# Plain attention steps that divide after the value products, with sums made by products with a block of ones, and a new table of order

## The chip, the cores and the metric

One core of a Trainium2 chip runs the program. The metric is the device time of one execution, in microseconds. Five engines work side by side, each on its own queue and in the order of that queue: PE (TensorE: matrix products; its weight loads are shown as PEld), DVE (VectorE), ACT (ScalarE), POOL (GpSimd) and SP (SyncE, which only issues transfers). They wait for each other by semaphores.

## The reference, cut to what matters

Causal attention with a bias from a running sum, and behind it a feed-forward layer whose hidden value is the largest of three products. B = 8 batches, H = 8 heads, S = 576 positions, D = 64; the feed-forward part has 4608 tokens, width 512 and 768 hidden values.

```python
scores = scale * np.matmul(q, k.transpose(0, 1, 3, 2))
s_pos = np.maximum(s, 0.0)
cum = np.cumsum(s_pos, axis=-1)
bias = -(cum[:, :, :, None] - cum[:, :, None, :])
scores = np.where(causal, -1000000000.0, scores + np.minimum(bias, 0.0))
scores = scores - np.max(scores, axis=-1, keepdims=True)
attn = np.exp(scores)
attn = attn / (np.sum(attn, axis=-1, keepdims=True) + 1e-09)
out = np.matmul(attn, v)
...
h = np.maximum(np.maximum(x @ w1, x @ w2), x @ w3)
return (h @ w_out).astype(np.float32)
```

## The kernel before

Heads go in pairs, one head on each half of the 128 partitions. A visit is one pair with some of its query blocks of 128 rows, and a step is one query block of one visit: 160 steps. The first four visits (v = 0 to 3, steps 0 to 7, query blocks 0 and 1 of batch 0) are the plain steps: they work in 32-bit floats throughout, with one product where all later steps split every number into two 16-bit halves and make three. The change touches the plain steps alone, besides the order.

One turn of the main loop, step t, puts on the queues: what is left of the probabilities of step t (`plain_probs`); the row maxima of step t+1 (`highest`, DVE, L771); the products of the feed-forward layer that are due; the scores of step t+2 (PE, L686 to L697); the exponentials of step t+1 (`expo`, ACT, L797, tiles e); and a list of other work for this step. In the plain steps these are, in the old code: the sums of the exponentials, which ACT collects beside L797 and rounds off at L803 (tile se); their reciprocal on DVE (L877, tile ri); two diagonal matrices with it (L880, ACT, tiles dg); products of the exponentials with them, which transpose and divide at once (L886, PE, tiles pp); a copy out of PSUM (L892, ACT, tiles p); the value products (L901, PE, into the accumulator av); and after each second step a copy of the result (L919, ACT) into x, the input of the feed-forward layer. L919 and its like are put off by a list, `pending`, that the next turn empties.

Beside the plain steps the weights of the feed-forward layer arrive (24 tiles of 512 KB, tiles r) and are unpacked from 64-bit floats by four operations: L1043 on ACT (tiles t), and L1047, L1051 and L1057 on DVE. `column_sums` then makes sums of them on PE (L1069), also into av; their largest value (L1077, tile amwu, DVE) leads by way of L536 to a scale, with which L1110 (ACT) and L1115 (DVE) split the weights into halves (tiles w). As soon as x is there, the up products of the first set (L1222, PE, tiles pm, in groups of 8 products), their maxima (L1234, DVE, tiles h) and the down products (L1244, PE, tiles po) run. All later sets run as L1142, L1159 and L1184.

The order of it all is written out by hand in a table, PLAN: `moved` shifts single pieces of work by whole steps, GROUPS says how many groups of feed-forward products run in the middle and at the end of each step, `fetched` when a weight is loaded, and KEEP adds products whose result nobody uses (`keep_on`, L928: weights identb, into av) at given steps.

Of the kernel before, what the change touches and what calls it, by code (L numbers as in the profile page):

```python
# [21 lines left out]
"moved": ({('later_keys',): 1, ('load', 10): 2, ('load', 4): -2, ('load', 5): -2, ('load', 6): -3, ('load', 7): -5, ('load_v',  # L22
19): -1, ('load_v', 20): 1, ('load_v', 24): 1, ('load_v', 29): 1, ('load_v', 32): 1, ('load_v', 34): 2, ('load_v',
37): 2, ('load_v', 5): -1, ('load_v', 7): -2, ('nat_bias', 18, 1): -1, ('nat_bias', 23, 0): -1, ('nat_bias', 30, 0):
1, ('nat_bias', 34, 0): 1, ('nat_bias', 38, 0): 2, ('nat_hi', 22, 0): -1, ('nat_hi', 25, 0): -1, ('nat_hi', 26, 1): 1,
('nat_hi', 30, 0): -1, ('nat_hi', 30, 1): 1, ('nat_hi', 34, 0): -1, ('nat_hi', 38, 0): -1, ('nat_hi', 38, 1): 1,
('nat_own', 21, 0, 0): 1, ('nat_own', 21, 0, 1): 2, ('nat_own', 21, 1, 0): 2, ('nat_own', 21, 1, 1): 2, ('nat_own',
22, 0, 0): 2, ('nat_own', 22, 0, 1): 1, ('nat_own', 25, 0, 0): 1, ('nat_own', 25, 0, 1): 1, ('nat_own', 25, 1, 0): 2,
('nat_own', 25, 1, 1): 1, ('nat_own', 26, 0, 0): 2, ('nat_own', 26, 0, 1): 1, ('nat_own', 26, 1, 0): 2, ('nat_own',
26, 1, 1): 1, ('nat_own', 29, 0, 0): 1, ('nat_own', 29, 0, 1): 1, ('nat_own', 29, 1, 0): 1, ('nat_own', 29, 1, 1): 2,  # L30
('nat_own', 30, 0, 1): 2, ('nat_own', 30, 1, 1): 2, ('nat_own', 33, 0, 0): 2, ('nat_own', 33, 0, 1): 1, ('nat_own',
33, 1, 1): 2, ('nat_own', 34, 0, 1): 2, ('nat_own', 34, 1, 0): 2, ('nat_own', 34, 1, 1): 2, ('nat_own', 37, 0, 1): 2,
('nat_own', 37, 1, 1): 2, ('nat_own', 38, 0, 0): 1, ('nat_own', 38, 0, 1): 1, ('nat_own', 38, 1, 0): 2, ('nat_own',
38, 1, 1): 1, ('pair_max', 20, 0): 1, ('pair_max', 21, 0): 2, ('pair_max', 22, 1): 1, ('pair_max', 23, 0): 2,
('pair_max', 23, 1): 1, ('pair_max', 24, 0): 1, ('pair_max', 24, 1): 1, ('pair_max', 25, 0): 1, ('pair_max', 27, 0):
1, ('pair_max', 28, 0): 1, ('pair_max', 28, 1): 1, ('pair_max', 29, 0): 2, ('pair_max', 30, 0): 3, ('pair_max', 30,
1): 3, ('pair_max', 31, 0): 1, ('pair_max', 31, 1): 1, ('pair_max', 32, 0): 1, ('pair_max', 33, 1): 1, ('pair_max',
34, 0): 2, ('pair_max', 34, 1): 3, ('pair_max', 35, 0): 2, ('pair_max', 36, 0): 1, ('pair_max', 36, 1): 1,
('pair_max', 37, 1): 1, ('pair_max', 38, 0): 2, ('pair_max', 38, 1): 2, ('pair_max', 39, 0): 2, ('pair_max', 39, 1):
1, ('pair_scale3', 3): 1, ('prep2', 10): 1, ('prep2', 9): -1, ('prep3', 5): -2, ('prep3', 7): 2, ('prep3', 8): -1,  # L40
('prep5', 11): 1, ('prep5', 15): -1, ('prep5', 17): -1, ('prep5', 18): -1, ('prep5', 4): -1, ('prep5', 7): -1,
('vmax', 20): 1, ('vmax', 21): 2, ('vmax', 22): 2, ('vmax', 24): 2, ('vmax', 25): 1, ('vmax', 26): 2, ('vmax', 30): 1,
('vmax', 32): 1, ('vmax', 33): 2, ('vmax', 34): 2, ('vmax', 36): 1, ('vmax', 37): 2, ('load_nat', 34): 1, ('decode4',
10): 1, ('prep3', 15): 1, ('nat_far', 29, 0, 1): -1, ('nat_far', 38, 0, 0): 1, ('nat_own', 24, 1, 1): 1, ('nat_bias',
37, 1): -1, ('nat_far', 23, 1, 1): -1, ('nat_own', 39, 0, 1): 1, ('nat_far', 24, 0, 1): -1, ('nat_far', 18, 1, 0): 1,
('load_nat', 31): 1, ('load_nat', 26): -2, ('nat_far', 38, 1, 0): 1, ('load_nat', 28): -2, ('nat_hi', 24, 0): 1,
('prep2', 0): -3, ('decode4', 21): 2, ('prep4', 22): -1, ('decode3', 17): -1, ('load_nat', 27): 1, ('nat_bias', 25,
1): 1, ('prep2', 11): 1, ('vmax', 39): 1, ('nat_bias', 22, 1): 2, ('load_v', 31): 1, ('load_nat', 36): -1,
('nat_bias', 35, 1): -2, ('nat_far', 35, 1, 1): 1, ('nat_bias', 38, 1): 1, ('nat_bias', 29, 1): 1, ('prep4', 24): -1,
('prep5', 14): -1, ('nat_hi', 16, 0): -1, ('prep5', 38): 1, ('nat_own', 31, 0, 1): 1, ('nat_hi', 28, 0): 1,  # L50
('nat_far', 32, 1, 0): -1, ('nat_far', 35, 0, 0): -1, ('bias4', 0): 1, ('prep4', 35): -2, ('load_w', 7): 1, ('nat_hi',
27, 0): -1, ('nat_bias', 24, 0): 2, ('prep3', 6): -1, ('prep5', 24): -1, ('load_nat', 35): -2, ('load_nat', 39): 1,
('nat_own', 35, 1, 0): 2, ('nat_hi', 33, 0): 1, ('nat_bias', 23, 1): 2, ('nat_far', 31, 1, 1): -1, ('prep4', 23): 1,
('nat_far', 29, 1, 0): -1, ('prep4', 15): -1, ('load_v', 22): -1, ('load_v', 10): 1, ('nat_far', 35, 1, 0): -2,
# [1526 lines left out]
```

## Time and profile before

| | |
|---|---|
| time before, median of 3 runs | 832.24 us (832.12 to 832.46) |
| the profiled execution: its time | 831.47 us |
| its span, first to last instruction | 829.7 us |
| PE busy | 799.0 us (96%) |
| PEld busy | 621.1 us (75%) |
| DVE busy | 634.9 us (77%) |
| ACT busy | 531.1 us (64%) |
| POOL busy | 299.2 us (36%) |
| mean granted TensorE clock | 0.991 |

An engine is busy while it works on an instruction. The shares are means over the whole span; which engine holds the others up has to be read stretch by stretch. The granted clock is the share of TensorE's full 2.4 GHz; its other level is 1.2 GHz, so that 0.66 over a stretch is a mixture of the two.

### The profile page before, as it was taken

How to read it: one execution, taken by the hardware profiler on the slowest of the kernel's cores; microseconds unless marked ns; L12 is line 12 of the kernel's file. 1: busy time of each engine (PE TensorE's matmuls, PEld its weight loads, DVE VectorE, ACT ScalarE, POOL GpSimd, SP SyncE). 2: the span in 40 equal slices, each digit the busy share in tenths (PEclk: the TensorE clock that was granted, in tenths of full speed). 3: DMA queues.
4: the chain of work that ended last, by engine and by line, in shares of the span. 5: the costliest groups of instructions: out<-in, count | busy, mean ns of one | idle time of the engine just before them, and what ended most of it. 6: DMA issues, size and time to landing. Idle time of an engine off the chain costs nothing.

```text
span 829.7 us, 20468 instructions
## 1 busy us (share of the span) xinstructions
PE 799.0 (96%) x7705; PEld 621.1 (75%) x7705; DVE 634.9 (77%) x1560; ACT 531.1 (64%) x1458; POOL 299.2 (36%) x531
## 2 busy tenths in 40 slices
...
GB/s 351 389 89 95 87 206 207 147 176 156 146 175 156 143 160 178 163 137 174 148 182 136 156 140 190 122 141 123 164 175 92 139 123 121 96 67 70 14 13 32
DMA packets 232387, 119.86 MB, mean 144 GB/s; under 512 B 204512, under 2 KB 213216, under 8 KB 232288
## 3 DMA queue, kind: packets, MB, share of 16 engines
...
q10 hardware_dynamic: 576, 1.57, 0.5%
...
## 4 chain that ended last, share of the span: by engine, by line
PE 85%; DVE 8%; ACT 3%; DMA 2%; issue 1%; DVEq 0%; ACTq 0%
PE pm L1142 47%; PE po L1184 15%; PE av L1008 8%; PE s L662 6%; DMA r<-in_w_dram 2%; PE pm L1222 2%; PE s L674 2%; DVE prl L855 1%; PE s L717 1%; DVE w L1115 1%; PE po L1244 1%; PE s L737 1%; ACT t L1043 1%; ACT prh L852 1%; DVE am L547 1%
## 5 line engine op out<-in xcount | busy, mean ns | idle before, releaser
L1142 PE MATMUL pm<-x,w 128*128 128x320 f16 (+1 forms) x3240 | 422.2, 287 | 2.4 <-ACT x L1018 0.7
L1142 PEld LDWEIGHTS <-w 128*128 128x128 f16 x3240 | 312.4, 98 | 91.9 <-issue 5.3
L1159 DVE SCALAR_TENSOR_TENSOR m<-pm,m 128x320 f32<-128x320 f32 (+1 forms) x180 | 81.7, 456 | 96.6 <-PE pm L1142 84.4
L1148 POOL CAST hh<-m 128x320 f16<-128x320 f32 (+1 forms) x90 | 46.7, 518 | 289.9 <-DVE m L1159 223.6
L852 ACT ACTIVATE prh<-e,ri 128x384 f16<-128x384 f32 (+2 forms) x192 | 91.1, 522 | 85.3 <-DVE ri L827 84.7
L1184 PE MATMUL po<-hh,w 128*128 128x320 f16 (+1 forms) x720 | 140.3, 287 | 0.0
L1184 PEld LDWEIGHTS <-w 128*128 128x128 f16 x1080 | 103.8, 98 | 29.6 <-issue 1.3
L766 DVE CUSTOM_DVE_ANT_0 s<-s,later,qf 128x128 f32<-128x128 f32 (+1 forms) x192 | 103.6, 550 | 9.5 <-PE s L662 6.8
L797 ACT ACTIVATE e<-s,nm 128x128 f32<-128x128 f32 (+4 forms) x216 | 105.4, 496 | 4.6 <-DVE nm L766 2.0
L855 DVE SCALAR_TENSOR_TENSOR prl<-e,ri,prh 128x384 f16<-128x384 f32 (+2 forms) x192 | 102.7, 575 | 3.1 <-ACT prh L852 2.2
L1184 PE MATMUL po<-hl,w 128*128 128x320 f16 (+1 forms) x360 | 103.2, 287 | 0.0
L276 POOL COPY lh<-fixed 64x576 f16<-64x576 f16 x96 | 73.6, 780 | 78.2 <-DVE fixed L251 76.2
L1156 ACT ACTIVATE m<-pm 128x320 f32<-128x320 f32 (+1 forms) x90 | 36.3, 403 | 73.7 <-PE pm L1142 71.6
L1149 POOL TENSOR_TENSOR hl<-m,hh 128x320 f16<-128x320 f32 (+1 forms) x90 | 69.6, 773 | 7.4
L662 PE MATMUL s<-lh 128*128 128x128 f16 (+3 forms) x384 | 67.1, 299 | 1.3 <-DVE prl L855 1.3
L1008 PEld LDWEIGHTS <-vh 128*64 128x64 f16 x1312 | 54.5, 111 | 11.9 <-issue 11.3
L1195 ACT ACTIVATE o<-po,os 128x320 f32<-128x320 f32 (+1 forms) x60 | 29.9, 498 | 50.1 <-PE po L1184 42.2
L797 ACT ACTIVATE s<-s,nm 128x512 f32<-128x512 f32 (+1 forms) x72 | 48.6, 674 | 0.0
L251 DVE SCALAR_TENSOR_TENSOR fixed<-fixed,qf,fixed 128x576 f16<-128x576 f32 x48 | 41.6, 902 | 6.3 <-ACT fixed L247 6.1
L662 PEld LDWEIGHTS <-lh 128*128 128x128 f16 x384 | 34.2, 98 | 15.5 <-POOL hl L1149 1.5
L797 ACT ACTIVATION_READ_ACCUMULATOR e<-s,nm 128x1 f32 x216 | 43.9, 203 | 0.0
L852 ACT ACTIVATE prh<-s,ri 128x512 f16<-128x512 f32 x48 | 30.3, 683 | 21.0 <-DVE ri L827 20.9
(196 smaller groups left out, 1184.4 us busy)
## 6 DMA issues: line engine op xcount, KB each, us to landing
...
```

Source lines behind the costliest of these rows:

```text
L276: nc.gpsimd.tensor_copy(out=R[v]["h"][own, j, x], in_=staged(v)[own, 3 - x])
L662: nc.tensor.matmul(ps[:, j, :nk], lhsT=w[:, c, qs], rhs=w[:, 1 - c, 0:nk], start=(x == "h" and not (lone and j)), stop=(x == "l"), skip_gr ...
L766: nc.vector.tensor_tensor_reduce(out=sc[:, j], in0=sc[:, j], in1=future[0][:, Q4 - nk:Q4], scale=n, scalar=3.0e38, op0=ALU.add, op1=ALU.mi ...
L797: nc.scalar.activation(out=to, in_=sc, func=AF.Exp, bias=nm[:, j:j + 1], scale=-1.0 if below(t) else 1.0, accum_out=sm[:, j:j + 1],)
L852: nc.scalar.activation(out=hi, in_=src, func=AF.Copy, scale=sc)
L855: nc.vector.scalar_tensor_tensor(out=lo, in0=src, scalar=sc, in1=hi, op0=ALU.mult, op1=ALU.subtract)
L1008: nc.tensor.matmul(o if ph else o.rearrange("p (i c) -> p i c", c=P), lhsT=lt, rhs=rt, start=(n < 2), stop=(n >= len(todo) - 2), skip_grou ...
L1142: nc.tensor.matmul(pm[:, :nq], lhsT=w[:, wt, kt, :], rhs=xt, start=(n == 0), stop=(n == 3 * NKT - 1))
L1148: nc.gpsimd.tensor_copy(out=st["hh"][:, ft, :nq], in_=m1[:, :nq])
L1149: nc.gpsimd.tensor_tensor(out=st["hl"][:, ft, :nq], in0=m1[:, :nq], in1=st["hh"][:, ft, :nq], op=ALU.subtract)
L1159: nc.vector.scalar_tensor_tensor(out=m1[:, :nq], in0=pm[:, :nq], scalar=HSC, in1=m1[:, :nq], op0=ALU.mult, op1=ALU.max)
L1184: nc.tensor.matmul(pm[:, :nq], lhsT=W[18 + ft][:, wt, dt, :], rhs=st[ht][:, ft, :nq], start=(n == 0), stop=(n == 3 * NFT - 1),)
```

## The change

In the plain steps the division moves behind the value products. ACT no longer collects sums beside the exponentials, and L803, L877 and L880 go. The products that transpose (pp) take the constant identity matrix in place of the diagonals. Behind the value products of each step, PE multiplies the same transposed probabilities by a block of ones of 64 columns (`pick`), which leaves the sums of each head in 64 rows of av, beside the values. ACT copies them, with 1e-9 added, into a tile rs (`norm`, put off as L919 was); after each second step DVE takes the reciprocal of rs over 256 columns and multiplies av by it into x (`out`), which takes the place of L919. KEEP is emptied, which takes out eight products, and some 55 entries of `moved`, GROUPS and `fetched` change by one or two steps, nearly all behind the plain steps. Line numbers behind the plain steps grow by eight.

```diff
--- before.py
+++ after.py
...
-"KEEP": ({('b', 37): 2, ('b', 70): 6}),
+"KEEP": ({}),
...
@@ -458,6 +461,10 @@
         nc.gpsimd.memset(blk[r, r], 1.0)
     one = const.tile([P, 1], BF16, name="one")
     nc.gpsimd.memset(one, 1.0)
+    pick = const.tile([P, D], F32, name="pick")
+    eps = const.tile([P, 1], F32, name="eps")
+    nc.gpsimd.memset(pick, 1.0)
+    nc.gpsimd.memset(eps, EPS)
     ones = const.tile([P, 2], F32, name="ones")
     nc.gpsimd.memset(ones, 0.0)
     sel = io.tile([HB, 1, 2, 160], F32R, tag="raw", name="sel", bufs=2)
@@ -780,8 +787,9 @@
     def expo(t):
         ps, nm, nk = U[t]
         nj = 2 if nk < S else 1
-        sm = small.tile([P, 2], F32, tag="sm", name=f"sm{t}")
         plain = steps[t][0] < NPA
+        if not plain:
+            sm = small.tile([P, 2], F32, tag="sm", name=f"sm{t}")
         away = not plain and aside(t)
         if away:
             E[t] = moe.tile([P, 2, 512], F32, tag="ex", name=f"e{t}", bufs=2)
@@ -796,11 +804,12 @@
                 to = E[t][:, j, :nk] if nj == 2 else E[t].rearrange("p j c -> p (j c)")[:, 0:S]
             nc.scalar.activation(
                 out=to, in_=sc, func=AF.Exp, bias=nm[:, j:j + 1], scale=-1.0 if below(t) else 1.0,
-                accum_out=sm[:, j:j + 1],
+                **({} if plain else dict(accum_out=sm[:, j:j + 1])),
             )
+        if plain:
+            return
         se = small.tile([P, 2], F32, tag="se", name=f"se{t}")
-        psc = 1.0 if plain else PSC
-        nc.scalar.activation(out=se[:, :nj], in_=sm[:, :nj], func=AF.Copy, scale=1.0 / psc, bias=EPS / psc)
+        nc.scalar.activation(out=se[:, :nj], in_=sm[:, :nj], func=AF.Copy, scale=1.0 / PSC, bias=EPS / PSC)
         SE[t] = (se, nj)
 
     PT = {}
@@ -871,26 +880,22 @@
     def plain_probs(t):
         v, qb = steps[t]
         U.pop(t)
-        se, _ = SE.pop(t)
         e = E.pop(t)
-        ri = small.tile([P, 2], F32, tag="ri", name=f"ri{t}")
-        nc.vector.reciprocal(out=ri, in_=se)
-        dg = att.tile([P, 2, P], F32, tag="vh", name=f"dg{t}")
-        for j in range(2):
-            nc.scalar.activation(out=dg[:, j], in_=ident, func=AF.Copy, scale=ri[:, j:j + 1])
         yield
         pm = ps_m.tile([P, 512], F32, tag="m", name=f"pp{t}")
         for kb in range(qb + 1):
             for j in range(2):
                 o = (2 * kb + j) * P
                 nc.tensor.matmul(
-                    pm[:, o:o + P], lhsT=e[:, j, kb * P:(kb + 1) * P], rhs=dg[:, j], start=True, stop=True
+                    pm[:, o:o + P], lhsT=e[:, j, kb * P:(kb + 1) * P], rhs=ident, start=True, stop=True
                 )
         yield
         PT[t] = att.tile([P, 512], F32, tag="prl", name=f"p{t}")
         n = 2 * (qb + 1) * P
         nc.scalar.activation(out=PT[t][:, :n], in_=pm[:, :n], func=AF.Copy)
         yield
+
+    RS = {}
 
     def plain_values(t):
         v, qb = steps[t]
@@ -902,25 +907,30 @@
                 av[:, qb * P:(qb + 1) * P], lhsT=R[v]["rv"][:, n % 2, n // 2, :], rhs=pT[:, n * P:(n + 1) * P],
                 start=(n == 0), stop=(n == 2 * qb + 1),
             )
-        if qb == 0:
-            return
+        sums = bank[:, 2 * P:3 * P]
+        for n in range(2 * (qb + 1)):
+            j = n % 2
+            nc.tensor.matmul(
+                sums[j * D:(j + 1) * D], lhsT=pick, rhs=pT[:, n * P:(n + 1) * P], start=(n < 2), stop=(n >= 2 * qb),
+                skip_group_check=True,
+            )
+
+        def norm():
+            if qb == 0:
+                RS[v] = att.tile([P, 2 * P], F32, tag="vl", name=f"rs{v}")
+            nc.scalar.activation(out=RS[v][:, qb * P:(qb + 1) * P], in_=sums, func=AF.Identity, bias=eps)
 
         def out():
             xt = x_tile(v, 0)
             X[b, 0].append(xt)
-            src = av[:, 0:PH[0][1]]
-            if (b, 0) not in PLAIN:
-                inv = VS[b, 0]
-                nc.scalar.activation(out=xt[:, 0], in_=src, func=AF.Copy, scale=inv)
-                nc.vector.scalar_tensor_tensor(
-                    out=xt[:, 1], in0=src, scalar=inv, in1=xt[:, 0], op0=ALU.mult, op1=ALU.subtract
-                )
-                return
-            nc.scalar.activation(out=xt, in_=src, func=AF.Copy)
+            nc.vector.reciprocal(out=RS[v], in_=RS[v])
+            nc.vector.tensor_tensor(out=xt, in0=av[:, 0:PH[0][1]], in1=RS.pop(v), op=ALU.mult)
             if g == NP - 1:
                 add_plain(b, 0)
 
-        pending.append(out)
+        pending.append(norm)
+        if qb:
+            pending.append(out)
 
 
     def keep_on(n, o=3 * P, w=P):
@@ -933,9 +943,7 @@
 
     def hold(place, t):
         n = KEEP.get((place, t), 0)
-        if t < 8:
-            keep_on(n, 2 * P)
-        elif t > max(scaled.values()) + 1:
+        if t > max(scaled.values()) + 1:
             keep_on(n)
         else:
             keep_on(n, 2 * P + D, D)
```

What DVE has in its queue in the third plain step (t = 2) before: row maxima nm, unpacking of two weights (t, r), the reciprocal ri of the next step.

```order
L771 TENSOR_REDUCE nm_286<-s_285 128x2
L1047 TENSOR_SCALAR t_305<-t_305 128x512
L1047 TENSOR_SCALAR t_307<-t_307 128x512
L1051 SCALAR_TENSOR_TENSOR r_258<-r_258,t_305 128x512
L1051 SCALAR_TENSOR_TENSOR r_155<-r_155,t_307 128x512
L1057 SCALAR_TENSOR_TENSOR r_258<-r_258 128x512
L1057 SCALAR_TENSOR_TENSOR r_155<-r_155 128x512
L877 RECIPROCAL ri_392<-se_342 128x2
L771 TENSOR_REDUCE nm_331<-s_330 128x2
```

And the same place in the changed kernel.

```order
L778 TENSOR_REDUCE nm_280<-s_279 128x2
L1055 TENSOR_SCALAR t_296<-t_296 128x512
L1055 TENSOR_SCALAR t_298<-t_298 128x512
L926 RECIPROCAL rs_277<-rs_277 128x256
L927 TENSOR_TENSOR x_0_321<-av,rs_277 128x256
L1059 SCALAR_TENSOR_TENSOR r_251<-r_251,t_296 128x512
L1059 SCALAR_TENSOR_TENSOR r_159<-r_159,t_298 128x512
L1065 SCALAR_TENSOR_TENSOR r_251<-r_251 128x512
L1065 SCALAR_TENSOR_TENSOR r_159<-r_159 128x512
L778 TENSOR_REDUCE nm_325<-s_324 128x2
```

The small reciprocal is gone and two operations over 256 columns stand ahead of the unpacking. ACT's queue at that place, of the changed kernel: the copy rs that the new reciprocal reads stands behind three unpacking operations, the third of which stood a step later before.

```order
L895 ACTIVATE p_290<-pp_272 128x512
L1051 ACTIVATE t_296<-r_251 128x512
L1051 ACTIVATE t_298<-r_159 128x512
L1051 ACTIVATE t_300<-r_253 128x512
L921 ACTIVATE rs_277<-av,eps 128x128
L805 ACTIVATE e_332<-s_279,nm_280 128x256 x2
```

In the old kernel this part of the queue held p, two unpackings, the two diagonals, the copy x and then the exponentials. The third place is DVE's queue at the end of the up products, before: splits of the down weights (w), a step's maxima and halves, the last maximum of the up products (h).

```order
L1115 SCALAR_TENSOR_TENSOR w_1198<-r_444,swd,w_1198 128x512
L1115 SCALAR_TENSOR_TENSOR w_1243<-r_726,swd,w_1243 128x512
L1115 SCALAR_TENSOR_TENSOR w_1200<-r_442,swd,w_1200 128x512
L827 RECIPROCAL ri_1317<-se_1292 128x1
L771 TENSOR_REDUCE nm_1278<-s_1277 128x2
L855 SCALAR_TENSOR_TENSOR pr_1319<-e_1290,ri_1317,pr_1319 128x512
L855 SCALAR_TENSOR_TENSOR pr_1319<-e_1290,ri_1317,pr_1319 128x64
L1234 TENSOR_TENSOR h_0_1_1027<-pm_0_5_2_1311,h_0_1_1027 128x256
```

And the same place in the changed kernel.

```order
L1123 SCALAR_TENSOR_TENSOR w_1223<-r_630,swd,w_1223 128x512
L1123 SCALAR_TENSOR_TENSOR w_1180<-r_485,swd,w_1180 128x512
L836 RECIPROCAL ri_1296<-se_1272 128x1
L778 TENSOR_REDUCE nm_1258<-s_1257 128x2
L864 SCALAR_TENSOR_TENSOR pr_1298<-e_1270,ri_1296,pr_1298 128x512
L864 SCALAR_TENSOR_TENSOR pr_1298<-e_1270,ri_1296,pr_1298 128x64
L1242 TENSOR_TENSOR h_0_1_1011<-pm_0_5_2_1290,h_0_1_1011 128x256
```

One split has moved from ahead of h to behind it.

## Rows read from the trace of the kernel before

**Rows 1.** The page, its first line.

```profile
span 829.7 us, 20468 instructions
```

**Rows 2.** Stretches: us, busy (count) of each engine, PEclk, DMA share, GB/s.

```profile
21.45:50.57 29.12, 21.10 (x194) 17.55 (x196) 26.37 (x58) 23.13 (x73) 0.00 (x0) 0.88 0.74 280
50.57:107.65 57.08, 52.32 (x327) 42.07 (x328) 53.30 (x126) 46.89 (x120) 5.58 (x5) 0.94 0.44 106
107.65:160.00 52.35, 50.05 (x509) 42.10 (x511) 46.28 (x83) 34.62 (x89) 27.60 (x41) 1.00 0.91 198
160.00:300.00 140.00, 136.60 (x1398) 100.72 (x1397) 119.09 (x278) 101.03 (x272) 62.50 (x113) 1.00 0.79 157
300.00:829.70 529.70, 526.29 (x5222) 409.15 (x5219) 375.42 (x987) 312.92 (x871) 199.46 (x347) 1.00 0.63 124
```

**Rows 3.** Chain of work that ended last: start us, us, what.

```profile
107.65 3.30 PE po L1244 x14
```

**Rows 4.** Waits of DVE from 21.45 to 50.57 us: total, times, longest.

```profile
DVE t L1047 <- ACT t L1043: 1.4, 3, 0.7
DVE nm L771 <- PE s L697: 0.8, 1, 0.8
```

**Rows 5.** Waits of PE from 10 to 52 us, the longest.

```profile
PE pp L886 <- ACT dg L880: 7.6, 6, 1.8
```

**Rows 6.** Timeline in the plain steps: start us, us, engine, line, operation, idle before.

```profile
20.74 1.24 ACT L1043 ACTIVATE t<-r 128x512 f32<-128x512 f32 x2 [0.81 <-DMA r<-in_w_dram]
...
21.45 0.99 DVE L1047 TENSOR_SCALAR t<-t 128x512 int32<-128x512 int32 x2 [0.34 <-ACT t L1043]
...
29.95 0.16 DVE L877 RECIPROCAL ri<-se 128x2 f32<-128x2 f32 x1
30.02 0.68 DVE L771 TENSOR_REDUCE nm<-s 128x2 f32<-128x512 f32 x1
```

**Rows 7.** Groups by shape, whole span: busy us, mean ns | idle before, releaser.

```profile
L827 DVE RECIPROCAL ri<-se 128x2 f32<-128x2 f32 x120 | 18.7, 156 | 9.8 <-ACT se L803 9.4
L827 DVE RECIPROCAL ri<-se 128x1 f32<-128x1 f32 x32 | 4.9, 153 | 1.6 <-ACT se L803 1.6
L1234 DVE TENSOR_TENSOR h<-pm,h 128x256 f32<-128x256 f32 x12 | 4.8, 418 | 0.1
L797 ACT ACTIVATE e<-s,nm 128x128 f32<-128x128 f32 x64 | 22.8, 368 | 0.9 <-DVE nm L771 0.9
L901 PE MATMUL av<-p,st 128*128 128x128 f32 x48 | 8.2, 313 | 0.3 <-ACT p L892 0.3
```

**Rows 8.** Timeline from the last column sums to the first up products.

```profile
49.93 0.53 PE L1069 MATMUL av<-one,r 128*128 128x1 bf16 x12 [1.75 <-ACT x L919]
...
50.57 0.23 DVE L1077 TENSOR_REDUCE amwu<-av 128x1 f32<-128x72 f32 x1 [0.24 <-PE av L1069]
...
51.52 4.73 PE L1222 MATMUL pm<-x,r 128*128 128x256 f32 x16
...
57.10 5.40 PE L1222 MATMUL pm<-x,r 128*128 128x256 f32 x24
```

**Rows 9.** Timeline at the first down products.

```profile
103.39 2.06 DVE L1115 SCALAR_TENSOR_TENSOR w<-r,swd,w 128x512 f16<-128x512 f32 x3
...
107.18 0.42 DVE L1234 TENSOR_TENSOR h<-pm,h 128x256 f32<-128x256 f32 x1
...
107.65 3.30 PE L1244 MATMUL po<-h,r 128*128 128x256 f32 x14 [1.25 <-DVE h L1234]
```

**Rows 10.** Timeline of PE at the products of KEEP.

```profile
202.85 0.27 PE L928 MATMUL av<-identb 128*128 128x128 bf16 x2
...
345.39 0.50 PE L928 MATMUL av<-identb 128*128 128x128 bf16 x6
345.73 0.81 PE L662 MATMUL s<-lh 128*128 128x384 f16 x4
```

**Rows 11.** Stretch with the first up products, columns as in rows 2.

```profile
50.00:55.00 5.00, 5.00 (x32) 4.36 (x32) 3.13 (x13) 3.10 (x9) 0.00 (x0) 0.66 0.47 187
```

More of the change, by code (lines that the diff above doesn't have):

```diff
@@ L51 @@
[L51 to L54, printed above, removed]
-('sign', 2): 1, ('sign', 15): 1, ('nat_bias', 26, 1): -1, ('nat_own', 23, 1, 1): 2, ('prep4', 27): -1, ('load_w', 5):
@@ new lines @@
+20, 0): 1, ('pair_max', 21, 0): 1, ('pair_max', 22, 1): 1, ('pair_max', 23, 0): 1, ('pair_max', 23, 1): 1,
+('pair_max', 24, 0): 1, ('pair_max', 24, 1): 1, ('pair_max', 25, 0): 1, ('pair_max', 27, 0): 1, ('pair_max', 28, 0):
+1, ('pair_max', 28, 1): 1, ('pair_max', 29, 0): 2, ('pair_max', 30, 0): 3, ('pair_max', 30, 1): 3, ('pair_max', 31,
+0): 1, ('pair_max', 31, 1): 1, ('pair_max', 32, 0): 1, ('pair_max', 33, 1): 1, ('pair_max', 34, 0): 2, ('pair_max',
+34, 1): 3, ('pair_max', 35, 0): 2, ('pair_max', 36, 0): 1, ('pair_max', 36, 1): 1, ('pair_max', 37, 1): 1,
@@ new lines @@
+-1, ('nat_far', 38, 0, 0): 1, ('nat_own', 24, 1, 1): 1, ('nat_bias', 37, 1): -1, ('nat_far', 23, 1, 1): -1,
+('nat_own', 39, 0, 1): 1, ('nat_far', 18, 1, 0): 1, ('load_nat', 31): 2, ('load_nat', 26): -2, ('nat_far', 38, 1, 0):
+1, ('load_nat', 28): -2, ('nat_hi', 24, 0): 1, ('prep2', 0): -3, ('decode4', 21): 2, ('prep4', 22): -1, ('decode3',
+17): -1, ('load_nat', 27): 1, ('nat_bias', 25, 1): 1, ('prep2', 11): 1, ('vmax', 39): 1, ('nat_bias', 22, 1): 2,
+('load_nat', 36): -1, ('nat_bias', 35, 1): -2, ('nat_far', 35, 1, 1): 1, ('nat_bias', 38, 1): 1, ('nat_bias', 29, 1):
@@ new lines @@
+1, ('prep4', 24): -1, ('prep5', 14): -1, ('nat_hi', 16, 0): -1, ('prep5', 38): 1, ('nat_own', 31, 0, 1): 2, ('nat_hi',
+28, 0): 1, ('nat_far', 32, 1, 0): -1, ('nat_far', 35, 0, 0): -1, ('bias4', 0): 1, ('prep4', 35): -3, ('load_w', 7): 1,
+('nat_hi', 27, 0): -1, ('nat_bias', 24, 0): 2, ('prep3', 6): -1, ('prep5', 24): -1, ('load_nat', 35): -2, ('load_nat',
+39): 1, ('nat_own', 35, 1, 0): 2, ('nat_hi', 33, 0): 1, ('nat_bias', 23, 1): 2, ('nat_far', 31, 1, 1): -1, ('nat_far',
+29, 1, 0): -1, ('prep4', 15): -1, ('load_v', 22): -1, ('nat_far', 35, 1, 0): -2, ('sign', 2): 1, ('sign', 15): 1,
@@ new lines @@
+-1, ('load_v', 17): -1, ('prep5', 9): -1, ('nat_hi', 24, 1): 1, ('nat_bias', 26, 0): 1, ('nat_own', 28, 1, 0): 1,
+('load_w', 13): 1, ('nat_far', 30, 1, 1): -1, ('nat_hi', 39, 0): 1, ('prep4', 14): -1, ('nat_far', 16, 0, 0): 1,
+('vmax', 35): -1, ('bias1',): 1, ('load_w', 12): -1, ('nat_far', 21, 1, 0): -1, ('nat_bias', 17, 0): -2, ('load_w',
+20): -2, ('nat_far', 16, 1, 0): -1, ('nat_far', 24, 1, 1): -1, ('nat_far', 32, 0, 1): -1, ('nat_hi', 27, 1): -1,
+('load_v', 4): -1, ('prep4', 25): -1, ('nat_bias', 22, 0): 1, ('load_nat', 30): 2, ('nat_hi', 35, 0): 1, ('load_w',
```

96 lines of the change are left out of this document (42 added, 54 removed), and 18 rows, old and new, of the table PLAN.

## The prediction

> **What bounds the kernel now.** The profiled execution took 831.47 us, 1.77 us more than its span of 829.7 us [rows 1] and 0.77 us less than the median of the runs, 832.24 us. I make the sum against the profiled execution and carry the difference over to the median.
>
> I read the table of stretches first. From 300 us on PE is busy for 526.29 of 529.70 us, and what is missing lies at the very end; from 160 to 300 us for 136.60 of 140, from 107.65 to 160 us for 50.05 of 52.35 [rows 2]. So from 107.65 us on the kernel is a queue of products with holes of 2.3 + 3.4 = 5.7 us before 300 us and none behind. Ahead of that it is DVE that is full: 53.30 of 57.08 us between 50.57 and 107.65 us, and 26.37 of 29.12 us between 21.45 and 50.57 us [rows 2], which are the plain steps from the third on. The chain of work agrees: it passes from DVE to PE at 107.65 us, at the first down products [rows 3]. A change in the plain steps therefore pays what it does to the time at which DVE gets through them, and only that.
>
> Then the waits. DVE lost 1.4 us to unpacked weights that ACT had not delivered and 0.8 us to scores that PE had not made [rows 4]; with small gaps its idle time there is 29.12 - 26.37 = 2.75 us. PE in turn waited 7.6 us for the diagonals [rows 5]. The timeline shows where transfers still set the pace: at 20.74 us ACT waited 0.81 us for a weight to land, and DVE for ACT behind it [rows 6]. Whatever is won before that is lost there, so I begin to count at 21.45 us.
>
> **The change part by part.**
>
> *PE: the sums.* 48 instructions are added (as many as L901 has), at most at L901's own price. Its 48 took 8.2 us in all [rows 7]; the new ones write the two heads to different halves of the rows and could overlap, so I bound them by half of that and all of it, 4.1 and 8.2 us. PE has 29.12 - 21.10 = 8.0 us free in this stretch alone [rows 2], and the wait for diagonals goes. They stand behind the value products, and what follows them on PE, pp of the next step, needs only exponentials that were made earlier. I put them at nothing; uncovered they would cost what exceeds the free time, which is little even at the upper bound.
>
> *ACT: less work.* Diagonals, accumulator reads, the rounding of sums and the copy x go; one copy of 128 columns a step comes, for which I take the 0.37 us of an exponential over as many columns [rows 7]. ACT was busy 23.13 of 29.12 us [rows 2] and gets freer. This is what takes away DVE's waits: scores no longer stand behind pp that waits for diagonals, and unpacking on ACT no longer behind them. I let all 2.75 us of DVE's idle time go.
>
> *DVE: more work.* Five small reciprocals go from the stretch, and each held the queue for 30.02 - 29.95 = 0.07 us [rows 6]: -0.35 us. Four times a reciprocal over 256 columns and a product over 256 columns come. The product reads PSUM just as L1234 does: 0.42 us [rows 7]. The trace shows no reciprocal of this width. Its own rows give 153 ns for one column and 156 ns for two [rows 7]; an operation that takes one column a clock comes to 0.42 us at 256, like L1234, and 3 ns a column would make 0.156 + 254 x 0.003 = 0.92 us. I take 0.42, the row that it is nearest to in shape, and keep 0.92 for the range. Two such operations overlap their neighbours by 0.09 us once (a reciprocal of 0.16 us holds the queue for 0.07): 0.42 + 0.42 - 0.09 = 0.75 us, four times 3.0 us.
>
> The Trainium skill ("VectorE: DVE Perf Modes", section "First, the fixed hardware budget") says that the engine's reciprocal is an iterative division with a repeat count of 8. If that meant eight passes for each column, the two rows above would lie some 8 ns apart and not 3; by the trace I do not read it so, and the third rival prices it.
>
> *A new wait.* In the third step the new reciprocal reads rs, which ACT makes behind three unpackings. They begin at 20.74 us when the weight lands; two take 1.24 us [rows 6], so three end at 20.74 + 3 x 0.62 = 22.60 us and rs at 22.97 us. DVE is free at 21.45 + 0.99 = 22.44 us [rows 6]: it waits 0.5 us, and the unpacking of weights is queued behind. In later steps ACT is ahead and the wait is nothing.
>
> Together DVE needs 26.37 - 0.35 + 3.0 + 0.5 = 29.5 us where it had 29.12: **+0.4 us** at 50.57 us. The bounds: without the wait 29.0 us, or -0.1; with the dear reciprocal 4 x 0.5 more, +2.4.
>
> *The end of the plain steps.* Before, the column sums waited 1.75 us for the copy x, and the largest value of them, amwu, followed on DVE [rows 8]. Now amwu stands behind the last pair of reciprocal and product in DVE's queue, which the sum contains. So the shift goes on whole to the scale, the weight splits and, through a DVE that stays full, to 107 us. I carry all of it.
>
> *One split less ahead of the last maximum.* Three splits took 2.06 us ahead of h, and PE waited 1.25 us for h [rows 9]. One of them moves behind: h comes 0.69 us earlier and PE's wait falls by as much: **-0.7 us**. If another hole behind it widens instead, nothing.
>
> *KEEP.* Six unused products held PE for 345.73 - 345.39 = 0.34 us [rows 10], eight so 0.45 us. They stand among products without a gap: **-0.45 us**. If they filled a hole, nothing.
>
> *The rest of the order.* Some 55 shifts by a step move work about in front of and behind PE's queue. Behind 300 us PE had no holes to close; before that there are 5.7 us. I cannot sign this from rows, take 0, and allow 2 us either way.
>
> Sum: +0.4 - 0.7 - 0.45 = -0.75 us, 830.7 us by the profiled execution, **831.5 us** as a median. I count 0.2% (1.7 us) as what a measurement of this kernel can tell from no change, so this is no change. Its own range is 829.8 to 833.2.
>
> **The rivals.**
>
> *The clock stays up (faster).* Between 50 and 55 us the granted clock was 0.66 [rows 11], after PE had waited for x; the first 16 up products took 4.73 us where the next 24 took 5.40 [rows 8], so 16 x (4.73/16 - 5.40/24) = 1.1 us were lost. The sums keep PE busier, and if the clock is at 2.4 GHz there, PE's products come 1.1 us sooner: 830.4 us. Against it: the last sums end before DVE has unpacked three weights, and PE then waits as before for the column sums' turn.
>
> *The new order closes holes (faster).* If half of the 5.7 us goes: 831.5 - 2.8 = 828.7 us. For it speaks that the shifts lie mostly where these holes are; against it that each moves a wait as easily as it removes one.
>
> *The reciprocal goes through eight times (slower).* L1234 against the small reciprocal gives (418 - 156)/254 = 1.03 ns a column [rows 7]; eight times that over 256 columns is 2.1 us, with the start 2.27, and four of them cost 4 x (2.27 - 0.42) = 7.4 us in a DVE that is full: 838.9 us. The rows at one and two columns speak against it. It decides above 0.42 + (1.7 + 0.75)/4 = 1.03 us a piece.
>
> *A wait in the new order (slower).* Several of rs, x or a weight stand later than they are wanted, such as the 0.5 us above in all four visits and a hole of 1 us behind: 834 us. It begins to count when DVE's idle time in the plain steps stays over 2 us.
>
> **How the numbers follow.** The forecast 0.46 (faster 0.07, same 0.36, slower 0.03), the clock 0.12 (faster 0.08, same 0.04), the order 0.20 (faster), the eightfold reciprocal 0.10 (slower), the wait 0.12 (same 0.03, slower 0.09). That makes faster 0.35, same 0.43, slower 0.22. Cases of both signs hold much of it, so the range reaches from the order's 828.7, a little beyond, to the wait's 834 with the dear reciprocal at 831.5 + 2.0 inside and some of the order's 2 us on top: 828.2 to 835.3. The eightfold reciprocal lies outside.
>
> **What the profile will show.** In the plain steps DVE busy for nearly the whole stretch, no wait of PE for ACT before pp, amwu within 1 us of 50.57 us, the wide reciprocal at about 0.42 us, PE's wait for h near 0.6 us, and no idle PE from 300 us on. I am wrong if the reciprocal takes 1 us or more, if amwu comes over 2 us earlier (then ACT and PE paced these steps and not DVE), or if the holes between 107 and 300 us change by more than 2 us.

## The result, and the profile after

The changed kernel takes 839.88 us in the median of four runs (839.03 to 840.82), the kernel before in the same comparison 832.18 us (831.70 to 832.46). The ratio is 1.0092 with a 95% interval of 1.0080 to 1.0103: slower by 0.9%, outside the range of the prediction. The profiled execution is the slowest of the four, 840.82 us.

First the span (line 1 of the page), then stretches of the changed kernel, with the columns of [rows 2]. The second border is where amwu comes; those behind it are borders of [rows 2] shifted by some 9.3 us.

```profile
span 839.0 us, 20508 instructions
```

```profile
21.45:58.61 37.16, 25.43 (x234) 20.26 (x230) 33.68 (x61) 19.77 (x52) 0.00 (x0) 0.83 0.62 238
58.61:116.90 58.29, 55.02 (x329) 43.60 (x330) 53.76 (x126) 46.74 (x118) 5.57 (x5) 0.90 0.44 93
116.90:169.30 52.40, 50.20 (x519) 42.27 (x519) 46.51 (x84) 33.66 (x87) 28.11 (x42) 1.00 0.93 196
169.30:309.30 140.00, 136.58 (x1395) 100.80 (x1392) 119.74 (x278) 101.15 (x272) 63.61 (x117) 1.00 0.80 160
309.30:839.00 529.70, 525.80 (x5209) 408.30 (x5206) 375.62 (x986) 312.61 (x870) 196.89 (x344) 1.00 0.62 123
```

Against [rows 2] the stretch up to amwu has grown from 29.12 to 37.16 us, by 8.04, and DVE's busy time in it from 26.37 to 33.68, by 7.31. The granted clock in the next stretch is lower (0.90 for 0.94), and PE's busy time behind it is the old one within 0.5 us. The lengths of the stretches behind amwu follow from the borders chosen, so they say nothing; what both traces have is the end of the first 24 down products:

```profile
114.31 5.41 PE L1252 MATMUL po<-h,r 128*128 128x256 f32 x24
```

Before, they came in a group of 10 and one of 14, which begins at 107.65 us [rows 9]:

```profile
104.02 2.38 PE L1244 MATMUL po<-h,r 128*128 128x256 f32 x10
```

The end is at 119.72 us now and was at 107.65 + 3.30 = 110.95 us. So of the 9.3 us in the span 8.0 arise in the plain steps, 0.7 from amwu to the end of these products and 0.5 behind them. The medians lie 7.7 us apart.

The groups by shape (busy us, mean ns, then idle before and its releaser) have the two operations that no row of before showed.

```profile
L836 DVE RECIPROCAL ri<-se 128x2 f32<-128x2 f32 x120 | 18.8, 156 | 8.0 <-ACT se L812 7.7
L926 DVE RECIPROCAL rs<-rs 128x256 f32<-128x256 f32 x4 | 7.0, 1751 | 2.1 <-ACT rs L921 2.1
L927 DVE TENSOR_TENSOR x<-av,rs 128x256 f32<-128x256 f32 x4 | 1.7, 425 | 0.4
L913 PE MATMUL av<-p,pick 128*64 128x128 f32 x48 | 5.2, 327 | 0.0
```

The reciprocal over 256 columns takes 1.75 us, not 0.42. The product takes 0.425 us and the sums on PE 5.2 us in all, both as put.

The waits of PE and of DVE from 21.45 to 58.61 us (total, times, longest):

```profile
PE av L1077 <- DVE x L927: 11.5, 4, 5.3
DVE rs L926 <- ACT rs L921: 2.1, 2, 1.5
DVE amwu L1085 <- PE av L1077: 0.7, 1, 0.7
```

PE's 7.6 us of waiting for the diagonals [rows 5] are gone, as predicted, and 11.5 us of another wait stand in their place: the column sums, which PE writes into columns 384 and up of av, wait for DVE's product, which reads columns 0 to 255 of it. The timeline shows the last of the four visits:

```profile
55.67 1.75 DVE L926 RECIPROCAL rs<-rs 128x256 f32<-128x256 f32 x1
57.52 0.42 DVE L927 TENSOR_TENSOR x<-av,rs 128x256 f32<-128x256 f32 x1
58.00 0.56 PE L1077 MATMUL av<-one,r 128*128 128x1 bf16 x12 [5.34 <-DVE x L927]
...
58.61 0.23 DVE L1085 TENSOR_REDUCE amwu<-av 128x1 f32<-128x72 f32 x1 [0.66 <-PE av L1077]
...
59.63 5.54 PE L1230 MATMUL pm<-x,r 128*128 128x256 f32 x16
```

Reciprocal, product, column sums and amwu follow one another here, and PE is idle for 5.34 us ahead of the last column sums, behind which the up products stand. These answer to [rows 8], where the column sums waited 1.75 us for ACT's copy. The Trainium skill ("PSUM — Partial Sum Buffer", section "PSUM bank collisions raise a hardware error ⚠️") says that two engines must not touch one bank of PSUM in the same partitions at once, at different columns either, and that semaphores have to guard it by bank. The trace agrees as far as it goes: the two stand in different columns of one tile, and PE waits 11.5 us for the product all the same. What would come without the wait no run shows.

### The profile page after: what moved, and what is told of

It reads as the page before. It is cut to its first block, busy times and chain, and to the rows that moved or that the text cites. A ratio compares the mean times of both kernels' runs of the same rounds, so it can differ in the third digit from the quotient of the medians.

```text
span 839.0 us, 20508 instructions
## 1 busy us (share of the span) xinstructions
PE 806.6 (96%) x7745; PEld 625.3 (75%) x7745; DVE 643.9 (77%) x1560; ACT 525.1 (63%) x1422; POOL 299.6 (36%) x533
## 4 chain that ended last, share of the span: by engine, by line
PE 80%; DVE 10%; ACT 4%; DMA 4%; issue 1%; POOL 0%; SPq 0%; ACTq 0%; DVEq 0%
PE pm L1150 43%; PE po L1192 16%; PE av L1016 7%; PE s L669 6%; DMA r<-in_w_dram 2%; PE s L681 1%; DVE prl L864 1%; PE s L724 1%; PE pm L1230 1%; PE po L1252 1%; DVE w L1123 1%; ACT prh L861 1%; DVE r L1065 1%; DVE r L1059 1%; DVE rs L926 1%
## 5 line engine op out<-in xcount | busy, mean ns | idle before, releaser
L599 POOL TENSOR_TENSOR qk<-raw,qk 128x576 fp32r<-128x576 f32 x8 | 12.4, 1555 | 92.2 <-ACT qk L590 92.1
```

## The experiments

Each ratio is that of a kernel to the kernel before in the runs of its own comparison, with its 95% interval; a time in us worked out from it takes 832.2 us for the kernel before.

**One-pass operation for the reciprocal.**

```diff
-            nc.vector.reciprocal(out=RS[v], in_=RS[v])
+            nc.vector.tensor_tensor(out=RS[v], in0=RS[v], in1=RS[v], op=ALU.max)
```

> The changed kernel, with the four wide reciprocals replaced by an operation of the same width that goes through once (the larger of rs and rs), so the division is left out. Price theory: DVE is full in the plain steps, and what was wrong is the 1.75 us that a reciprocal over 256 columns takes where I had put 0.42. Four times 1.33 = 5.3 us go, amwu comes at 58.6 - 5.3 = 53.3 us or, if the waits behind the reciprocals shrink too, near 51, and the time is 832 to 834.6. Bank theory: PE's column sums waiting for the product that reads av (11.5 us) are a cost of their own, by the late sums and scores behind them; the waits stay, shortened by 1.33 us each, DVE goes on waiting over 2 us for rs and the time is 835 to 837. Order theory (the table of order costs the time): 839 or more.

Measured 834.01 us (832.69 to 836.35), 1.0014 (1.0003 to 1.0024). The operation took 424 ns and amwu came at 52.95 us. The difference to the changed kernel is (1.0092 - 1.0014) x 832.2 = 6.5 us of the 7.7. That is what the price theory said, and the order theory falls. Waits of the same kind stay, shorter, and DVE still waits for rs, as the bank theory had it:

```profile
PE av L1077 <- DVE x L927: 6.6, 2, 4.0
...
DVE rs L926 <- ACT rs L921: 1.9, 2, 1.3
```

**Copy out of PSUM first.**

```diff
+            nc.scalar.activation(out=xt, in_=av[:, 0:PH[0][1]], func=AF.Copy)
             nc.vector.reciprocal(out=RS[v], in_=RS[v])
-            nc.vector.tensor_tensor(out=xt, in0=av[:, 0:PH[0][1]], in1=RS.pop(v), op=ALU.mult)
+            nc.vector.tensor_tensor(out=xt, in0=xt, in1=RS.pop(v), op=ALU.mult)
```

> The changed kernel, but ACT first copies av out of PSUM into x, and DVE multiplies x by the reciprocal there; PE's column sums then have only ACT's copy to wait for, while the reciprocals keep their 1.75 us. Price theory: DVE needs as long as before, the time stays within 1 us of 839.9, at 839 to 840. Bank theory: PE's 11.5 us of waiting for the product fall to 2 us or less, DVE's 2.1 us of waiting for rs and the 5.3 us of idle PE ahead of the first up products go with them, and the time is 836 to 837.5. Order theory: 839 to 840.

Measured 837.61 us (837.01 to 838.02), 1.0058 (1.0044 to 1.0072): 2.8 us faster than the changed kernel, below what the price theory alone allowed. The waits from 21.45 to 56.5 us, of PE and of DVE, show why:

```profile
PE av L906 <- ACT p L895: 4.2, 3, 1.8
PE av L1078 <- ACT x L926: 3.0, 1, 3.0
...
DVE rs L927 <- ACT rs L921: 0.6, 1, 0.6
```

The wait for the product is gone; PE waits 3.0 us for ACT's copy and 4.2 us for p in its place, and DVE's waiting for rs falls from 2.1 to 0.6 us: the 1.47 us of it in the seventh step came by way of PE, which had stood at the column sums and made the sums late. (Its clock had a part in that, as the run with the old order shows below.) amwu comes at 56.53 us instead of 58.61. So the wait for the bank is a cost of its own, beside the price. Its size is less sure: against a second measurement of the changed kernel (below, 1.0086) it is 2.3 us in place of 2.8, and the intervals then overlap.

**Both edits together.**

```diff
+            nc.scalar.activation(out=xt, in_=av[:, 0:PH[0][1]], func=AF.Copy)
-            nc.vector.reciprocal(out=RS[v], in_=RS[v])
-            nc.vector.tensor_tensor(out=xt, in0=av[:, 0:PH[0][1]], in1=RS.pop(v), op=ALU.mult)
+            nc.vector.tensor_tensor(out=RS[v], in0=RS[v], in1=RS[v], op=ALU.max)
+            nc.vector.tensor_tensor(out=xt, in0=xt, in1=RS.pop(v), op=ALU.mult)
```

> The changed kernel with both of the first two edits: the wide reciprocals replaced by an operation of the same width that goes through once (the division is left out), and av copied out by ACT before DVE multiplies. This is the kernel that my prediction's sum was made for: 0.42 us a piece, and column sums that wait for a copy on ACT. If price and bank are all that was wrong, it comes to 831.5, within 1 us (0.998 to 1.000 of the kernel before), and amwu within 1 us of 50.6. If the two causes only cover each other (the waits are a consequence of the dear reciprocal), it stays where the one-pass kernel was, at 1.001, some 833.5. If a third cost is hidden, over 834.

Measured 832.42 us (831.52 to 833.81), 1.0007 (0.9998 to 1.0016), amwu at 51.67 us. This is the kernel that my sum was for. The sum had 831.5, 0.9991 of the kernel before: 1.3 us short by the ratios, and the lower end of the interval still lies 0.6 us above it. Price and bank together are (1.0092 - 1.0007) x 832.2 = 7.1 us. Of what is left, part is in the plain steps, where amwu comes 0.7 us behind the 50.57 + 0.4 us of my sum and DVE waits 1.4 us for rs in place of 0.5:

```profile
DVE rs L927 <- ACT rs L921: 1.4, 2, 0.8
```

The rest is in the terms of the order (below). The expectation that two causes would explain all but 1 us came true by the median (832.42 for 831.5) and was just missed by the ratio (0.998 to 1.000 was put) and by amwu (1.1 us from 50.57). Without the bank wait the price is (1.0058 - 1.0007) x 832.2 = 4.2 us, with it 6.5; by amwu it is 4.9 and 5.7 us; worked out it was 4 x 1.33 = 5.3. That they cost more together than alone would fit, as the product that PE waits for stands behind the reciprocal, but the four intervals hardly tell it. With the cheap operation the bank wait is worth 0.6 us (1.0014 against 1.0007), which the intervals do not separate from nothing. So the other expectation, that the waits cost something only behind the dear reciprocal, is not ruled out by the times; amwu, at 51.67 us against 52.95, speaks against it.

**The order alone.** The table of the changed kernel, with the old arithmetic of the plain steps. The edit is the part of the diff on PLAN (in the section on the change its last line stands):

```diff
-"KEEP": ({('b', 37): 2, ('b', 70): 6}),
+"KEEP": ({}),
```

> The kernel before with the new table of order (its KEEP, which is empty, too), and the old arithmetic of the plain steps. Price and bank theory: within 1.5 us of the kernel before, 831 to 833; if the smaller wait for the last maximum h and the eight products are what I put them at, 831. Order theory: the table costs several us, 836 or more.

Measured 831.16 us (829.25 to 834.07), 0.9982 (0.9970 to 0.9994): faster than both kernels, by 0.18% against the one before. With the old arithmetic the order costs nothing. Its stretch up to amwu, and below it that of the kernel with both edits:

```profile
21.45:47.96 26.51, 22.44 (x194) 18.68 (x196) 25.52 (x57) 22.56 (x72) 0.00 (x0) 0.81 0.77 295
```

```profile
21.45:51.67 30.22, 24.55 (x222) 19.52 (x221) 28.20 (x61) 20.55 (x55) 0.00 (x0) 0.83 0.76 292
```

In the upper one DVE idles 0.99 us where it idled 2.75 before [rows 2], with the old arithmetic. Here the new order took that idle time away, which I had credited to a freer ACT (with the old order and the new arithmetic it goes as well, below). The two kernels have one order, and DVE is busy 28.20 - 25.52 = 2.68 us longer in the lower one; my own terms for it, -0.35 + 3.0, give 2.65.

And DVE and PE at the first down products, with the order alone:

```profile
100.71 1.40 DVE L1118 SCALAR_TENSOR_TENSOR w<-r,swd,w 128x512 f16<-128x512 f32 x2
...
103.61 0.95 DVE L858 SCALAR_TENSOR_TENSOR pr<-e,ri,pr 128x512 f16<-128x512 f32 x2 [0.58 <-ACT pr L855]
104.48 0.42 DVE L1237 TENSOR_TENSOR h<-pm,h 128x256 f32<-128x256 f32 x1
...
104.95 3.30 PE L1247 MATMUL po<-h,r 128*128 128x256 f32 x14 [1.26 <-DVE h L1237]
```

One split stands less ahead of h, as I had read from the order, and PE waits 1.26 us for h where it waited 1.25 [rows 9]: in the place of the split DVE now waits 0.58 us for pr from ACT. The first 24 down products end at 104.95 + 3.30 = 108.25 us, 2.70 us earlier than before, and the span of this execution, 828.6 us, is only 1.1 us shorter. Two waits of PE for transfers took most of the rest, which are not in the trace of before:

```profile
207.14 0.33 PE L665 MATMUL s<-lh 128*128 128x128 f16 x3 [0.58 <-DMA lh<-fixed]
...
511.94 0.36 PE L1011 MATMUL av<-pl,vh 128*64 128x256 f16 x4 [0.94 <-DMA pl<-prl]
```

**The change with the old order.** The changed arithmetic, with the old table.

```diff
-"KEEP": ({}),
+"KEEP": ({('b', 37): 2, ('b', 70): 6}),
```

> The changed arithmetic with the old table of order and its eight unused products. Price and bank theory: as slow as the changed kernel or slower, 839 to 842, with the same four reciprocals of 1.75 us. Order theory: near the kernel before, 832 to 834.

Measured 838.42 us (838.19 to 840.24), 1.0071 (1.0058 to 1.0084), a little under what was put. The loss is there without the new order. Against the changed kernel's 1.0092 (1.0080 to 1.0103) the intervals overlap, so whether the old order suits the dear reciprocal better is not told by the times. amwu comes at 57.09 us where it came at 58.61, and DVE waits 0.5 us for rs where it waited 2.1. The column sums ahead of the seventh step and the reciprocal in it, with the stretch between, first in this kernel and then in the changed one:

```profile
35.78 0.66 PE L1074 MATMUL av<-one,r 128*128 128x1 bf16 x16 [2.61 <-DMA raw<-in_start_dram]
42.91 1.75 DVE L923 RECIPROCAL rs<-rs 128x256 f32<-128x256 f32 x1 [0.23 <-ACT rs L918]
36.00:44.00 8.00, 7.80 (x66) 6.09 (x63) 7.73 (x15) 4.33 (x11) 0.00 (x0) 0.79 0.63 246
```

```profile
35.83 0.66 PE L1077 MATMUL av<-one,r 128*128 128x1 bf16 x16 [2.63 <-DVE x L927]
44.42 1.75 DVE L926 RECIPROCAL rs<-rs 128x256 f32<-128x256 f32 x1 [1.47 <-ACT rs L921]
36.00:44.00 8.00, 8.00 (x56) 6.41 (x54) 6.79 (x14) 3.39 (x7) 0.00 (x0) 0.57 0.63 243
```

PE stood equally long at the column sums and then worked at another granted clock, 0.79 against 0.57, with the same instructions in its queue. So the wait of 1.47 us needs the lower clock besides the standing; why the clock was lower in this execution, and whether the order has a part in it, stays open.

**The old order with both edits.**

```diff
-"KEEP": ({}),
+"KEEP": ({('b', 37): 2, ('b', 70): 6}),
...
+            nc.scalar.activation(out=xt, in_=av[:, 0:PH[0][1]], func=AF.Copy)
-            nc.vector.reciprocal(out=RS[v], in_=RS[v])
-            nc.vector.tensor_tensor(out=xt, in0=av[:, 0:PH[0][1]], in1=RS.pop(v), op=ALU.mult)
+            nc.vector.tensor_tensor(out=RS[v], in0=RS[v], in1=RS[v], op=ALU.max)
+            nc.vector.tensor_tensor(out=xt, in0=xt, in1=RS.pop(v), op=ALU.mult)
```

> The old table of order and its eight products with the changed arithmetic, the wide reciprocal replaced by an operation that goes through once (the division is left out) and av copied out by ACT first. This is the part of my sum without the order: +0.4 us on the kernel before, with bounds -0.1 and +2.4 that held a dearer reciprocal, 832.2 to 832.9, 1.0000 to 1.001. Under the new order the same edits gave 1.0007. If old and new order differ here as they do with the old arithmetic (0.998), this one comes to 1.002; if as with the dear reciprocal (the old order was the faster by 1.5 us), to 0.999.

Measured 833.34 us (832.21 to 834.81), 1.0015 (1.0006 to 1.0024), 1.2 us where the sum had 0.4, inside its bounds. The intervals of this and of 1.0007 under the new order overlap. The stretch up to amwu:

```profile
21.45:50.65 29.20, 23.31 (x242) 18.86 (x242) 28.15 (x62) 19.81 (x55) 0.00 (x0) 0.94 0.79 303
```

amwu comes at 50.65 us where it came at 50.57 before, and DVE idles 29.20 - 28.15 = 1.05 us in place of 2.75, with the old order: the freer ACT does take away idle time, as I had put it. The first 24 down products end at 111.02 us, 0.07 us later than before. So what this kernel loses beyond the sum it loses behind them, where its code is that of the kernel before.

**Half the columns**, with the changed kernel once more beside it:

```diff
-            nc.vector.reciprocal(out=RS[v], in_=RS[v])
+            nc.vector.reciprocal(out=RS[v][:, 0:P], in_=RS[v][:, 0:P])
```

> The changed kernel with the reciprocal over the first 128 of the 256 columns alone (the other half is left undivided): 0.95 us a piece in place of 1.75. Price theory: four times 0.80 = 3.2 us less on a full DVE, 836.7 where the changed kernel has 839.9, half of what the one-pass kernel gave back. If the cost comes from the reciprocal standing there at all (the wait for rs, the order of the queue) and not from its length, within 1 us of 839.9.

> The changed kernel once more, beside the other two on one chip, as what they are compared with: 839 to 840.8, 1.008 to 1.010 of the kernel before.

Measured 835.07 us (833.99 to 835.98), 1.0032 (1.0021 to 1.0044), beside 838.78 us (837.67 to 842.57), 1.0086 (1.0066 to 1.0106), which gives a second trace of the changed kernel, with amwu at 58.76 us. The reciprocals took 948 ns. Four times 1751 - 948 = 803 ns are 3.2 us; the medians differ by 3.7 us, the ratios by 4.5 us. The time follows the length of the reciprocal; whether by a little more than its own sum, the intervals do not tell.

**Reciprocals by themselves**, in the kernel before, near its end:

```diff
+    wide = att.tile([P, 512], F32, tag="prl", name="wide")
+    nc.vector.memset(wide, 2.0)
+    for n in (2, 16, 64, 128, 256, 512):
+        nc.vector.reciprocal(out=wide[:, :n], in_=wide[:, :n])
+    nc.vector.reciprocal(out=wide[0:D, 0:256], in_=wide[0:D, 0:256])
+    nc.vector.tensor_tensor(out=wide[:, 0:256], in0=wide[:, 0:256], in1=wide[:, 0:256], op=ALU.max)
+    nc.gpsimd.tensor_tensor(out=wide[:, 0:256], in0=wide[:, 0:256], in1=wide[:, 0:256], op=ALU.mult)
```

> The kernel before, with reciprocals over 2, 16, 64, 128, 256 and 512 columns of a scratch tile added on DVE near the end, where DVE has little to do, one of 256 columns on 64 partitions, an operation of 256 columns that goes through once, and a product of 256 columns on POOL. Price theory: a straight line of some 6.3 ns a column from 0.16 us at 2 columns, so 0.24, 0.54, 0.94, 1.75 and 3.37 us, and 1.75 us on half the partitions as well. If the 1.75 us came from something beside them in the plain steps (another engine at the same memory, the sums just written), the 256 columns here take 0.42 to 0.9 us.

Groups by shape, busy us and mean ns:

```profile
L1519 DVE RECIPROCAL wide<-wide 128x512 f32<-128x512 f32 x1 | 3.4, 3353 | 0.0
L1519 DVE RECIPROCAL wide<-wide 128x256 f32<-128x256 f32 x1 | 1.8, 1753 | 0.0
L1520 DVE RECIPROCAL wide<-wide 64x256 f32<-64x256 f32 x1 | 1.7, 1745 | 0.0
L1519 DVE RECIPROCAL wide<-wide 128x128 f32<-128x128 f32 x1 | 1.0, 953 | 0.0
L1519 DVE RECIPROCAL wide<-wide 128x64 f32<-128x64 f32 x1 | 0.6, 553 | 0.0
L1521 DVE TENSOR_TENSOR wide<-wide 128x256 f32<-128x256 f32 x1 | 0.4, 424 | 0.0
L1519 DVE RECIPROCAL wide<-wide 128x16 f32<-128x16 f32 x1 | 0.3, 253 | 0.0
L1519 DVE RECIPROCAL wide<-wide 128x2 f32<-128x2 f32 x1 | 0.2, 166 | 0.0
```

It is a straight line of (3353 - 253)/496 = 6.25 ns a column, about six times the 1.03 ns a column that the prediction worked out for L1234, and it takes as long on half the partitions as well. Nothing beside the reciprocal makes it dear. Between one and two columns the rows of before differed by 3 ns [rows 7]; two points so close together say nothing of the line.

**The division on POOL.**

```diff
+            nc.scalar.activation(out=xt, in_=av[:, 0:PH[0][1]], func=AF.Copy)
-            nc.vector.reciprocal(out=RS[v], in_=RS[v])
-            nc.vector.tensor_tensor(out=xt, in0=av[:, 0:PH[0][1]], in1=RS.pop(v), op=ALU.mult)
+            nc.gpsimd.tensor_tensor(out=RS[v], in0=RS[v], in1=minus.to_broadcast([P, 2 * P]), op=ALU.pow)
+            nc.gpsimd.tensor_tensor(out=xt, in0=xt, in1=RS.pop(v), op=ALU.mult)
```

> The changed kernel with the division off DVE: ACT copies av into x, POOL, which is idle in the plain steps, raises rs to the power -1 and multiplies x by it. Price theory: eight operations leave a full DVE, 4 x (1.75 + 0.42) = 8.7 us; if POOL has each pair done within the 10 us from one visit to the next, the time falls to 831 or below, 829 to 831, and amwu comes near 49 us. Bank theory: PE's column sums wait for ACT's copy alone, so nothing is left of the 11.5 us beyond 3. Against both: a power on POOL that takes 10 us or more makes x late at the first up products and the time 835 or more, or POOL's work slows DVE's beside it, which the rows of the unpacking would show as longer than 0.69 us each.

Measured 969.94 us (968.87 to 972.32), 1.1664 (1.1645 to 1.1684). The tile's instructions, shortest, median and longest in ns:

```profile
L929 POOL TENSOR_TENSOR rs<-rs,minus x4: 41117/41120/41637, 23.8 to 149.9; 128x256 f32<-128x256 f32 x4
L930 POOL TENSOR_TENSOR x<-x,rs x4: 723/724/724, 65.5 to 191.1; 128x256 f32<-128x256 f32 x4
```

This is the case that the expectation set against both theories, and it decides nothing between them. A power on POOL takes 41 us for 256 columns, four of them set the pace up to 191 us, and the up products wait. An engine with free time is of no use for an operation that is 23 times as long there as on DVE (41.1/1.75).

**KEEP alone.** The kernel before with KEEP empty.

```diff
-"KEEP": ({('b', 37): 2, ('b', 70): 6}),
+"KEEP": ({}),
```

> The kernel before with KEEP empty and nothing else changed: eight products less on PE. My prediction's term for it is -0.45 us, 832.0 where the kernel before has 832.4. If they filled a hole it is the same as before; if they kept the clock up, slower by 0.5 or more.

Measured 831.72 us (830.89 to 834.24), 0.9998 (0.9988 to 1.0008). The expected -0.45 us would be 0.9995; the interval holds that and nothing too, so this term stays open.

## Why the prediction was wrong, point by point

**What bounds the kernel** was right: DVE in the plain steps, at the rate of one to one. What amwu lost, 8.04 us, is in the span at the end, with 0.7 us up to the first down products and 0.5 us behind them on top. In ten of the twelve traces of this document without the division on POOL, the first 24 down products end 60.3 to 60.4 us after amwu begins, whatever stood ahead of it; the other two have 61.1 (the changed kernel) and 61.2 (half the columns).

**DVE: more work.** Here the prediction failed, in one number: "0.42, the row that it is nearest to in shape". A reciprocal is no one-pass operation; it took 1.75 us, and 0.92, the bound above it, was made from the same two rows of one and two columns, so that the range had no room for it either. All else of this step held: 2.68 us measured where 2.65 were put, with the one-pass operation.

The rule of the Trainium skill that I weighed against these rows and set aside ("VectorE: DVE Perf Modes", section "First, the fixed hardware budget") was the better guide. Its repeat count of 8, read as eight passes for a column, gives an estimate of 8 x 1.03 = 8.2 ns; the widths show 6.25, and the measurement decides.

**The new wait.** The wait for rs in the third step was 0.60 us where I put 0.5, in part by luck: in the second trace of the changed kernel it was 1.18 us, as ACT itself waited there for the sums on PE. The one in the seventh step, 1.47 us (0.92 in the second trace), I missed.

**The end of the plain steps.** I saw that `out` takes the place of L919 and that amwu stands behind it on DVE. I did not draw the other half: the column sums on PE waited for L919 [rows 8], so now they wait for the reciprocal and product of a full DVE, in all four visits, with the next value products and sums queued behind them. This is the second step that failed, worth 2.8 us with the dear reciprocal (2.3 by the second measurement). What I named as the sign of success, "no wait of PE for ACT before pp", came true and says nothing: it is the wait that goes, not the one that comes.

**ACT: less work.** The freer ACT takes idle time away as put, with the old order: from 2.75 us to 1.05, of which 0.54 us are the new wait for rs. But the new order by itself takes away as much (0.99 us left), and the two do not add: with both edits under the new order DVE idles 30.22 - 28.20 = 2.02 us, of which 1.4 us are for rs.

**One split less** came out at nothing, the other bound that the text named: 0.58 us of waiting for ACT moved into its place. In the changed kernel itself PE comes to the down products so late, at 114.31 us, that it does not wait for h at all.

**KEEP** stays open, and **the rest of the order**, put at 0 with 2 us either way, belongs to a table that as a whole gave (0.9982 - 1) x 832.2 = -1.5 us with the old arithmetic. The holes of PE between 107 and 300 us stayed as they were: 2.20 + 3.42 = 5.6 us in the changed kernel, 5.7 before.

**PE: the sums** held: 5.2 us between the bounds of 4.1 and 8.2, covered by PE's idle time.

**The rivals.** The eightfold reciprocal, at 838.9 us, came nearest, and its point of decision, 1.03 us a piece, was passed. But it got there by two errors that cancel: 2.27 us a piece for 1.75, and no wait for the bank. That the clock stays up was turned round: after 5.34 us of idle PE the granted clock from 55 to 65 us was 0.66, and the first 16 up products took 5.54 us where they had 4.73 [rows 8]. A second stretch at the lower clock lies ahead of the down products (0.69; in the second trace of the changed kernel it was 0.89 there):

```profile
55.00:65.00 10.00, 7.00 (x37) 5.90 (x38) 6.79 (x19) 5.48 (x16) 0.00 (x0) 0.66 0.13 52
105.00:115.00 10.00, 9.87 (x44) 7.11 (x44) 9.16 (x21) 8.84 (x20) 0.77 (x1) 0.69 0.61 115
```

But this clock does not set the time. The kernel before with KEEP emptied, whose plain steps and up products are those of before without a change, had in its profiled execution:

```profile
49.52 0.53 PE L1069 MATMUL av<-one,r 128*128 128x1 bf16 x12 [0.47 <-ACT x L919]
50.17 0.23 DVE L1077 TENSOR_REDUCE amwu<-av 128x1 f32<-128x72 f32 x1 [0.32 <-PE av L1069]
50.72 3.68 PE L1222 MATMUL pm<-x,r 128*128 128x256 f32 x16
...
105.03 5.50 PE L1244 MATMUL po<-h,r 128*128 128x256 f32 x24
```

The 16 products took 1.05 us less than before, almost the 1.1 us of this rival, and the down products end 110.53 - 50.17 = 60.36 us after amwu, where it was 110.95 - 50.57 = 60.38. What PE wins here it does not carry to the down products, as DVE is the full engine on the way (53.30 of 57.08 us [rows 2]). With the order alone the same 16 products took 3.68 us too; as the old order shows the same in one execution and not in another, that is no merit of the order.

**A wait in the new order** had its sign, over 2 us of idle DVE: 37.16 - 33.68 = 3.48 us in the changed kernel, 2.1 of them for rs. By itself, with the one-pass operation and the early copy, the kernel stayed at 832.42 us, below the 834 us of this rival.
